# Three row blocks at once at the opening of the product of w3 and w_out2

## The chip, the cores and the metric

One Trainium2 chip, one core. The metric is the device time of one execution in microseconds, the median of several runs. Profiles show one execution; their times count from the first instruction. TensorE, VectorE, ScalarE, GpSimd and SyncE are PE, DVE, ACT, POOL and SP in the rows, PEld is TensorE's weight load.

## The reference

```python
attn_out = _attn_ref(q, k, v, g_q, g_k)     # 4 batches, 12 heads, 448 tokens, 64 wide; RMS norm on q and k, softmax
x = attn_out.transpose(0, 2, 1, 3).reshape(1792, 768)
x = relu(x @ moe_w_in) ** 2 @ moe_w_out     # 768 -> 2048 -> 768
a, b = x @ w1, x @ w2                       # 768 -> 1024
out = ((a * b) @ w3) @ w_out                # w3 1024 x 1024, w_out 1024 x 768
```

q, k and v are float32. The weights are float64 in memory.

## The kernel before

The two last products are one: w3 and the last w_out (wo2 in the code) are multiplied first, w3o = w3 @ w_out2, and each batch then uses w3o. The kernel goes through the 48 heads one after another (4 batches of 12), and beside each head's attention it issues matmuls of a second stream, paced by a credit: during heads 0 to 12 these are the 384 matmuls of w3o, and afterwards, for each batch, the 1008 matmuls of its MoE layers. The function fill(n) adds n to the credit and draws steps of three matmuls from a generator (gen_w3o, then gen_moe) until the credit is used. There are six such calls in a head. After head 12 the rest of w3o is drawn, and the first batch's MoE begins.

Products are made with numbers split in two: a float32 value is a high part (a rounded copy) and a low part (the value less the high part), and mm3 issues three matmuls, high by high, high by low, low by high (lines 262 to 264).

A weight comes in units of 128 partitions by 384 or 512 columns. The list `units` gives their order, and every step on a unit runs through the list in this order: load (SyncE; a float64 unit goes into one of four raw64 buffers, line 180), words (the high word on ScalarE, line 194, the low word on GpSimd or ScalarE, lines 198 and 200), join (VectorE makes a float32 of both, line 207, and frees the raw64 buffer), split_hi (ScalarE, line 106) and split_lo (GpSimd or VectorE, line 114). Which engine does the low word and the low part goes by the unit's number modulo 3 and 5 in the w3o product. advance(u) brings all of these up to unit u and a few units beyond: low parts to u + 2, high parts one unit further, joins to two and words to three units beyond the low parts, loads to five.

For w3o the units are 16 of w3 (two for each of 8 row blocks, four 128 x 128 pieces each) and 16 of wo2 (8 pieces jc by two halves of the columns, 384 wide). gen_w3o makes one row block after another, first half 0 of its columns, then half 1. The first row block therefore brings all 16 wo2 units with it, and these stay: two in the pool of x, eight in that of act, six in that of x2. Those of w3 go through the pool hl with four buffers. The sum of a row block and half, eight steps, is in a PSUM buffer of the pool ps_mm, which has three. ScalarE copies it to one of two osb buffers (copy_on, line 106), and SyncE stores that to w3o (line 289).

The order of instructions on each engine is made when the program is built, by a scheduler that follows the program's order where it expects operands to be ready and goes around what it expects to wait. On the chip each engine then keeps its order.

At the start SyncE issues the loads of the first k and q group, q_t of heads 0 to 2, v of heads 0 and 1 and the first two units; all later units follow with the first call of fill.

Of the kernel before, what the change touches and what calls it, by code (L numbers as in the profile page):

```python
# [8 lines left out]
F32 = mybir.dt.float32  # L9
F32R = mybir.dt.float32r  # L10
# [19 lines left out]
def attention_moe_kernel(  # L30
# [22 lines left out]
    NE = w_out.shape[0] // 4  # L53
    KF = w_out.shape[2] // 64
    NJ = w1.shape[0] // 2
    NIC = w3t.shape[0] // 2
    HC = KX * 128 // 2
    ENGS = {"v": nc.vector, "g": nc.gpsimd}
    KCS = ((0, 128), (128, 128), (256, 128), (384, 64))
# [44 lines left out]
    def copy_on(eng, out, in_):  # L104
        if eng == "a":
            nc.scalar.activation(out=out, in_=in_, func=AF.Copy)  # L106
        elif eng == "g":
            nc.gpsimd.tensor_scalar(out=out, in0=in_, scalar1=1.0, scalar2=1.0, op0=ALU.mult, op1=ALU.mult)
        else:
            nc.vector.tensor_copy(out=out, in_=in_)  # L110
# [10 lines left out]
    units = []  # L121
    wo_at, w3_at = {}, {}

    def add_wo(half, g):
        for j in range(NIC // 2):
            jc = g * NIC // 2 + j
            wo_at[half, jc] = len(units)
            units.append((wo2[jc, half], None))

    def add_w3(i):  # L130
        w3_at[i] = len(units)
        units.append((w3t[i], None))

    add_w3(0)
    add_wo(0, 0)
    add_w3(1)
    add_wo(0, 1)
    add_wo(1, 0)
    add_wo(1, 1)
    for i in range(2, 2 * NIC):  # L140
        add_w3(i)
    U0 = len(units)
    wo_units = set(wo_at.values())
    def two_first(n, on=True):
# [42 lines left out]
    def load_to(i):  # L187
        while pos["load"] <= min(i, NU - 1) and is64(pos["load"]):
            load_next()
# [27 lines left out]
    def split_hi(i):  # L217
        n = units[i][0].shape[-1]
        if i in wo_units:
            k = pos["wo"]  # L220
            pos["wo"] += 1
            p, nm = (xp, "x") if k < 2 else ((actp, "act") if k < 10 else (x2p, "x2"))
            t = p.tile([128, 2, S], F32R, name=nm, tag=nm)
        else:
            t = hlp.tile([128, 2, 512], F32R, name="hl", tag="hl")
        copy_on("a", t[:, 0, :n], raws[i][:, :n])
        hls[i] = t
# [27 lines left out]

    def use(u):
        advance(u)
        return hls.pop(u).rearrange("p a (k m) -> p a k m", m=128)

    def mm3(ps, w, wk, x, i, n):  # L260
        last = n - 1
        nc.tensor.matmul(ps, w[:, 0, wk, :], x[0], start=(i == 0), stop=False)  # L262
        nc.tensor.matmul(ps, w[:, 0, wk, :], x[1], start=False, stop=False)  # L263
        nc.tensor.matmul(ps, w[:, 1, wk, :], x[0], start=False, stop=(i == last))  # L264

    def hl_pair(t, n=S):
        return (t[:, 0, :n], t[:, 1, :n])
# [2 lines left out]
    wo = {}  # L270

    def gen_w3o():
        for ic in range(NIC):
            ws = None
            for half in range(2):
                ps = ps_mm.tile([128, 512], F32, name="mm", tag="mm")
                for jc in range(NIC):
                    if ws is None or jc * 2 // NIC >= len(ws):
                        ws = (ws or []) + [use(w3_at[2 * ic + len(ws or [])])]
                    if ic == 0:  # L280
                        advance(wo_at[half, jc])
                        wo[half, jc] = hls.pop(wo_at[half, jc])
                    w = ws[jc * 2 // NIC]
                    mm3(ps[:, :HC], w, jc % (NIC // 2), hl_pair(wo[half, jc], HC), jc, NIC)
                    yield 3
                o = t2.tile([128, S], F32, name="osb", tag="osb")
                copy_on("a", o[:, :HC], ps[:, :HC])
                k, c = divmod(ic, NIC // 2)
                nc.sync.dma_start(
                    out=w3o.rearrange("(e k) p (c m) -> e k p c m", k=2, m=128)[half * 3:half * 3 + 3, k, :, c, :]  # L290
                    .rearrange("e p m -> p e m"),
                    in_=o[:, :HC].rearrange("p (e m) -> p e m", m=128),
                )


    xs = {}
# [364 lines left out]
    nc.sync.dma_start(out=g_sb, in_=g_in)  # L661
    load_group(0)
    load_head(1)
    make_identity(nc, ident)
    nc.vector.tensor_copy(out=ident_r, in_=ident)
    nc.vector.scalar_tensor_tensor(
# [7 lines left out]
    start_fill(gen_w3o(), W3O)  # L674
    first.close()
    for h in range(NH + 1):
        n = W3O / ((H + 1) * 6) if h <= H else MOE / (H * 6)
        load_head(h + 3)
        load_v(h + 1)
        if h % GH == 0:  # L680
            load_group(h // GH + 1)
        stage_qk(h, 0)
        fill(n)
        stage_exp(h, 0)
        if h % H != 1:
            stage_x(h - 2)
        stage_t(h - 1, 0)
        stage_t(h - 1, 1)
        fill(n)
        stage_lo(h - 1)  # L690
        if h < NH:
            v_prep(h)
        fill(n)
        stage_k(h + 1)
        stage_t(h - 1, 2)
        stage_t(h - 1, 3)
        fill(n)
        stage_lo(h - 1)
        stage_qk(h, 1)
        fill(n)  # L700
        stage_exp(h, 1)
        fill(n)
        stage_v(h - 1)
        if h % GH == 1:
            group_prep(h // GH + 1)
        head_prep(h + 2)
        if h and h % H == 0:
            fill(1e9)
            stage_x(h - 1)
            start_fill(gen_moe(h // H - 1), MOE)  # L710
# [57 lines left out]
```

## Time and profile before

| | us |
|---|---|
| median of 3 runs | 1234.7 |
| lowest and highest | 1232.09, 1235.27 |
| the profiled execution | 1234.55 |
| its span, first to last instruction | 1232.8 |

The span leaves out 1.75 us around the instructions. The profiled execution lies 0.15 us under the median.

### The profile page before, as it was taken

The numbers are of one execution on the slowest core, as the hardware profiler recorded it, in microseconds if no ns is written. First come the engines' busy times: TensorE is split into PE (matmuls) and PEld (weight loads), VectorE is DVE, ScalarE is ACT, GpSimd is POOL, SyncE is SP. The second block draws the span as 40 slices with busy tenths as digits, with TensorE's granted clock in tenths as the row PEclk, the third lists the DMA queues.
The fourth block names the chain that finished last, engine by engine and source line by source line (L and its number), as shares of the span: only waits on it lengthen the run. The fifth ranks groups of instructions, "written<-read, shape, count | busy, mean of one in ns | idle before, by whom it ended". The sixth has DMA issues, their size and how long they took to land.

```text
span 1232.8 us, 18950 instructions
## 1 busy us (share of the span) xinstructions
PE 1160.9 (94%) x6192; PEld 1049.3 (85%) x6192; DVE 709.7 (58%) x1314; ACT 728.5 (59%) x1553; POOL 781.3 (63%) x772
## 2 busy tenths in 40 slices
PE   3789999998989899999999999999999999999998
PEld 2578888886878789998998998999999999999998
DVE  6699879768978774646567555655664421012100
ACT  5889876767657565656645555656545554343342
POOL 5875534655676655766776764856766556678673
PEclk9999999999998999999999999999999999999999
DMA  7774557888888755555535455544544443333342
GB/s 218 244 238 151 165 146 226 276 283 264 251 264 257 234 180 179 146 148 145 151 118 161 139 169 158 143 142 127 154 123 120 138 138 113 107 116 102 104 125 75
DMA packets 111347, 207.63 MB, mean 168 GB/s; under 512 B 12208, under 2 KB 66704, under 8 KB 111248
## 3 DMA queue, kind: packets, MB, share of 16 engines
q1 hardware_dynamic: 107792, 200.92, 54.0%
q10 hardware_dynamic: 3456, 5.51, 1.2%
q8 instruction: 49, 0.80, 0.3%
q14 instruction: 50, 0.41, 0.1%
HBM read 149.95 MB, written 27.53 MB: 144 GB/s over the span
## 4 chain that ended last, share of the span: by engine, by line
PE 60%; DMA 4%; DVE 2%; POOL 2%; ACT 1%; issue 1%; SPq 0%; DVEq 0%; POOLq 0%; ACTq 0%
PE mm L262 17%; PE mm L263 17%; PE mm L264 17%; PE kv L622 3%; PE pt L570 3%; DMA raw<-w 2%; DMA pw<-p 2%; PE sc L525 1%; PE sc L524 1%; POOL hl L114 1%; DVE raw L207 1%; PE kv L508 1%; PE mm L611 0%; ACT p L543 0%; POOL x L114 0%
## 5 line engine op out<-in xcount | busy, mean ns | idle before, releaser
L114 POOL TENSOR_TENSOR hl<-raw,hl 128x384 fp32r<-128x384 f32 (+1 forms) x383 | 446.4, 1169 | 258.5 <-ACT hl L106 253.3
L106 ACT ACTIVATE hl<-raw 128x384 fp32r<-128x384 f32 (+1 forms) x416 | 233.7, 564 | 147.6 <-PE mm L264 85.6
L263 PE MATMUL mm<-x,hl 128*128 128x448 f32 (+1 forms) x832 | 306.2, 368 | 8.6 <-POOL x L114 8.6
L262 PE MATMUL mm<-x,hl 128*128 128x448 f32 (+1 forms) x832 | 310.5, 373 | 3.8 <-ACT x L106 1.8
L264 PE MATMUL mm<-x,hl 128*128 128x448 f32 (+1 forms) x832 | 305.7, 367 | 4.5 <-POOL hl L114 2.6
L263 PE MATMUL mm<-act,hl 128*128 128x448 f32 (+1 forms) x640 | 234.4, 366 | 3.3 <-POOL act L114 3.2
L262 PE MATMUL mm<-act,hl 128*128 128x448 f32 (+1 forms) x640 | 236.9, 370 | 0.0
L264 PE MATMUL mm<-act,hl 128*128 128x448 f32 (+1 forms) x640 | 233.6, 365 | 0.7 <-DVE hl L114 0.7
L543 ACT ACTIVATE p<-sc,nb,rr 112x448 f32<-112x448 f32 x192 | 137.4, 719 | 86.4 <-DVE nb L527 83.0
L263 PEld LDWEIGHTS mm<-x,hl 128*128 128x128 f32 x832 | 158.1, 190 | 22.1 <-POOL x L114 10.2
L264 PEld LDWEIGHTS mm<-x,hl 128*128 128x128 f32 x832 | 158.2, 190 | 19.0 <-POOL hl L114 4.0
L262 PEld LDWEIGHTS mm<-x,hl 128*128 128x128 f32 x832 | 157.9, 190 | 18.5 <-ACT x L106 3.3
L526 DVE TENSOR_REDUCE nb<-sc 112x1 f32<-112x448 f32 x192 | 113.1, 615 | 35.6 <-PE sc L525 34.3
L263 PEld LDWEIGHTS mm<-act,hl 128*128 128x128 f32 x640 | 121.0, 189 | 14.3 <-POOL act L114 4.8
L264 PEld LDWEIGHTS mm<-act,hl 128*128 128x128 f32 x640 | 120.9, 189 | 10.6 <-DVE hl L114 1.1
L262 PEld LDWEIGHTS mm<-act,hl 128*128 128x128 f32 x640 | 121.0, 189 | 9.4
L114 DVE TENSOR_TENSOR ptr<-pt,ptr 128x448 fp32r<-128x448 f32 x144 | 87.1, 619 | 72.0 <-ACT ptr L106 71.4
L200 POOL TENSOR_SCALAR raw<-raw 128x384 uint32<-128x384 uint16 (+1 forms) x110 | 82.1, 747 | 73.0 <-DMA raw<-w_in 18.8
L207 DVE SCALAR_TENSOR_TENSOR raw<-raw 128x384 uint32<-128x384 uint32 (+1 forms) x120 | 84.8, 711 | 39.8 <-POOL hl L114 25.2
L194 ACT ACTIVATE raw<-raw 128x384 f32<-128x384 f32 (+1 forms) x120 | 70.5, 597 | 53.9 <-DMA raw<-w 18.0
L114 POOL TENSOR_TENSOR act<-gf,act 128x448 fp32r<-128x448 f32 x80 | 97.4, 1218 | 7.2 <-DVE gf L334 3.0
L334 DVE TENSOR_TENSOR gf<-mm,r 128x448 f32<-128x448 f32 x64 | 39.8, 621 | 94.4 <-ACT r L330 93.9
(82 smaller groups left out, 1588.7 us busy)
## 6 DMA issues: line engine op xcount, KB each, us to landing
pw<-p SPq DMA_DIRECT2D x72, 392.0 KB, 4.3
raw<-f_in SPq DMA_DIRECT2D x96, 192.0 KB, 2.4
raw<-f_out SPq DMA_DIRECT2D x72, 256.0 KB, 2.7
raw<-f SPq DMA_DIRECT2D x96, 192.0 KB, 2.4
raw<-w_in SPq DMA_DIRECT2D x32, 384.0 KB, 4.5
raw<-w_out SPq DMA_DIRECT2D x24, 512.0 KB, 6.1
raw<-w SPq DMA_DIRECT2D x32, 384.0 KB, 4.9
raw<-w3o SPq DMA_DIRECT2D x48, 256.0 KB, 2.7
```

Of the source, the lines that this page charges most:

```text
L106: nc.scalar.activation(out=out, in_=in_, func=AF.Copy)
L114: e.tensor_tensor(out=out, in0=in0, in1=in1, op=ALU.subtract)
L194: nc.scalar.activation(out=hi, in_=hi, func=AF.Prelu, scale=2.0**-112, alpha=-(2.0**32))
L200: nc.gpsimd.tensor_scalar(out=t[:, :n, 0], in0=low, scalar1=2.0**-13, scalar2=2.0**-14 - 0.5, op0=ALU.mult, op1=ALU.add)
L207: nc.vector.scalar_tensor_tensor(out=f[:, :n].bitcast(U32), in0=t[:, :n, 1], scalar=3, in1=t[:, :n, 0], op0=ALU.logical_shift_left, op1=AL ...
L262: nc.tensor.matmul(ps, w[:, 0, wk, :], x[0], start=(i == 0), stop=False)
L263: nc.tensor.matmul(ps, w[:, 0, wk, :], x[1], start=False, stop=False)
L264: nc.tensor.matmul(ps, w[:, 1, wk, :], x[0], start=False, stop=(i == last))
L334: nc.vector.tensor_tensor(out=gf, in0=ps, in1=r, op=ALU.mult)
L526: nc.vector.tensor_reduce(out=nb[:, j:j + 1], in_=o[j], axis=AX.X, op=ALU.max, negate=True)
L543: nc.scalar.activation(out=p, in_=o[j], func=AF.Exp, scale=d["rq"][:, c:c + 1], bias=nb[:, j:j + 1], accum_out=sm[:, i, c:c + 1],)
L570: nc.tensor.transpose(to[:kn, c * P:(c + 1) * P], d["p"][c][:, k0:k0 + kn], one)
```

## The change

The w3o product opens with three row blocks at once. For half 0 of the columns, step jc of rows 0, 1 and 2 follow each other, so one wo2 unit serves nine matmuls instead of three; then the same for half 1; rows 3 to 7 follow one by one as before. The units stand in the order in which this uses them: w3 units of three rows between the wo2 units of half 0, then the wo2 units of half 1, then the other w3 rows. Rows 0 and 1 are cut into units of 3, 3 and 2 pieces, the other rows in 4 and 4, which makes 34 units. The six units of rows 0 and 1 go to the pool of x, the wo2 units to act (eight), x2 (six) and x (two). Units 2 and 3 are loaded right after q_t of head 1. The credit is 4.5 for each call in heads 0 and 1 and 5.0 for each in heads 2 to 12, instead of 4.92 in all.

```diff
-    NIC = w3t.shape[0] // 2
+    NIC = w3t.shape[0]
+    NR = 3
...
+    def add_w3(ic, a, b):
+        for jc in range(a, b):
+            w3_at[ic, jc] = (len(units), jc - a)
+        units.append((w3t[ic][:, a * 128:b * 128], None))
+
+    CUTS = [(0, 3, 6, 8)] * (NR - 1) + [(0, 4, 8)] * (NIC - NR + 1)
+    for jc in range(NIC):
+        for ic in range(NR):
+            if jc in CUTS[ic][:-1]:
+                add_w3(ic, jc, CUTS[ic][CUTS[ic].index(jc) + 1])
+            if ic == 0:
+                add_wo(0, jc)
+    for jc in range(NIC):
+        add_wo(1, jc)
+    early = {w3_at[ic, jc][0] for ic in range(NR - 1) for jc in range(NIC)}
+    for ic in range(NR, NIC):
+        for a, b in zip(CUTS[ic], CUTS[ic][1:]):
+            add_w3(ic, a, b)
...
-            p, nm = (xp, "x") if k < 2 else ((actp, "act") if k < 10 else (x2p, "x2"))
+            p, nm = (actp, "act") if k < 8 else ((x2p, "x2") if k < 14 else (xp, "x"))
             t = p.tile([128, 2, S], F32R, name=nm, tag=nm)
+        elif i in early:
+            t = xp.tile([128, 2, S], F32R, name="x", tag="x")
...
+        ws = {}
+
+        def rows(ics, half):
+            pss = [ps_mm.tile([128, 512], F32, name="mm", tag="mm") for _ in ics]
+            for jc in range(NIC):
+                for ic, ps in zip(ics, pss):
+                    u, i = w3_at[ic, jc]
+                    if u not in ws:
+                        ws[u] = use(u)
                     if ic == 0:
                         advance(wo_at[half, jc])
                         wo[half, jc] = hls.pop(wo_at[half, jc])
+                    mm3(ps[:, :HC], ws[u], i, hl_pair(wo[half, jc], HC), jc, NIC)
+                    if jc == NIC - 1:
+                        o = t2.tile([128, S], F32, name="osb", tag="osb")
+                        copy_on("a", o[:, :HC], ps[:, :HC])
...
                     yield 3
+
+        for half in range(2):
+            yield from rows(range(NR), half)
+        for ic in range(NR, NIC):
+            for half in range(2):
+                yield from rows([ic], half)
...
     load_head(1)
+    load_to(3)
...
-        n = W3O / ((H + 1) * 6) if h <= H else MOE / (H * 6)
+        n = (9 * NR if h < 2 else (W3O - 18 * NR) / (H - 1)) / 6 if h <= H else MOE / (H * 6)
...
-        "w3t": units(w3.T, 4),
+        "w3t": units(w3.T, 8),
```

## Rows read from the trace of the kernel before

**Rows 1.** Head of the page: the span, and each engine's busy time.
```profile
span 1232.8 us, 18950 instructions
...
PE 1160.9 (94%) x6192; PEld 1049.3 (85%) x6192; DVE 709.7 (58%) x1314; ACT 728.5 (59%) x1553; POOL 781.3 (63%) x772
```

**Rows 2.** Windows: stretch, length, busy us and instructions by engine, clock, DMA, GB/s.
```profile
5.00:10.00 5.00, 0.49 (x4) 0.49 (x4) 3.05 (x12) 2.47 (x5) 2.77 (x4) 1.00 1.00 311
...
core 0: us, PE busy (x) PEld busy (x) DVE busy (x) ACT busy (x) POOL busy (x), PEclk, DMA share, GB/s
...
20.00:60.00 40.00, 26.01 (x104) 19.00 (x105) 25.38 (x41) 31.02 (x68) 33.87 (x37) 0.96 0.70 223
60.00:100.00 40.00, 36.02 (x218) 31.67 (x216) 39.37 (x69) 35.81 (x76) 28.68 (x31) 1.00 0.68 218
...
190.00:460.00 270.00, 242.97 (x1269) 215.75 (x1268) 217.63 (x383) 175.21 (x381) 166.08 (x179) 0.97 0.79 249
460.00:1232.80 772.80, 767.40 (x4079) 704.05 (x4077) 335.15 (x599) 404.84 (x858) 502.92 (x459) 1.00 0.45 134
```

**Rows 3.** Waits from 20 to 60 us: us in total, times, longest.
```profile
PE mm L263 <- POOL x L114: 5.9, 3, 2.9
...
DVE nb L526 <- PE sc L525: 8.0, 6, 2.0
```

**Rows 4.** Timeline of TensorE: start, duration; L524 is a head's scores.
```profile
32.99 0.57 PE L524 MATMUL sc<-kt,qh 128*112 128x448 f32 x1
...
56.19 0.43 PE L524 MATMUL sc<-kt,qh 128*112 128x448 f32 x1
...
58.33 0.34 PE L262 MATMUL mm<-act,hl 128*128 128x384 f32 x1
...
59.29 0.44 PE L264 MATMUL mm<-x,hl 128*128 128x384 f32 x1 [0.45 <-POOL hl L114]
...
59.74 0.34 PE L263 MATMUL mm<-x,hl 128*128 128x384 f32 x1
59.92 0.35 PE L264 MATMUL mm<-x,hl 128*128 128x384 f32 x1
...
97.25 0.38 PE L524 MATMUL sc<-kt,qh 128*112 128x448 f32 x1
```

**Rows 5.** SyncE: issues of loads in order of time, and its waits from 10 to 70.
```profile
14.56 0.35 SPq L414 DMA_DIRECT2D qt<-q_t  x1
14.96 1.37 SPq L180 DMA_DIRECT2D raw<-wo  x3
...
25.32 10.08 SPq L180 DMA_DIRECT2D raw<-wo  x6
...
62.89 2.03 SPq L180 DMA_DIRECT2D raw<-w3t  x2
...
SPq L180 <- DVE raw L207: 35.7, 18, 6.8
```

**Rows 6.** Windows of one line: L262 (one for each step), then L207 (joins).
```profile
0.00:56.18 56.18, 7.46 (x16) 3.83 (x16) 0.97 0.75 234
...
0.00:56.18 56.18, 13.29 (x19) 0.97 0.75 234
0.00:97.20 97.20, 21.59 (x29) 0.98 0.72 225
```

**Rows 7.** Groups of VectorE from 60 to 100: count, busy us, mean ns.
```profile
L207 DVE SCALAR_TENSOR_TENSOR raw<-raw 128x512 uint32<-128x512 uint32 x9 | 7.6, 846 | 0.2 <-ACT raw L198 0.2
...
L114 DVE TENSOR_TENSOR hl<-raw,hl 128x512 fp32r<-128x512 f32 x2 | 2.0, 1000 | 0.0
```

**Rows 8.** Joins up to 100 us: ns least, median, most; starts; forms.
```profile
L207 DVE SCALAR_TENSOR_TENSOR raw<-raw x29: 544/678/1297, 10.3 to 96.2; 128x384 uint32<-128x384 uint32 x16, 128x512 uint32<-128x512 uint32 x13
```

**Rows 9.** Timelines of ScalarE and GpSimd: the first exponential, the first use of v.
```profile
18.99 0.72 ACT L543 ACTIVATE p<-sc,nb,rr 112x448 f32<-112x448 f32 x1 [5.68 <-DVE nb L527]
...
17.16 1.58 POOL L114 TENSOR_TENSOR vhl<-v,vhl 128x256 fp32r<-128x256 f32 x2 [1.78 <-DVE nt L432]
```

**Rows 10.** First result of w3o: copy, issue of its store, time to landing.
```profile
41.67 0.49 ACT L106 ACTIVATE osb<-mm 128x384 f32<-128x384 f32 x1 [0.62 <-PE mm L264]
...
44.81 0.43 SPq L289 DMA_DIRECT2D w3o<-osb  x1
...
w3o<-osb SPq DMA_DIRECT2D x1, 192.0 KB, 3.8
```

More of the change, by code (lines that the diff above doesn't have):

```diff
@@ L122, in attention_moe_kernel, with add_wo @@
     wo_at, w3_at = {}, {}
[L124 to L141, printed above, removed]
+    def add_wo(half, jc):
+        wo_at[half, jc] = len(units)
+        units.append((wo2[jc, half], None))
+    def add_w3(ic, a, b):
[15 more added lines that the diff above has]
+            add_w3(ic, a, b)
     U0 = len(units)
@@ L257, in use @@
         advance(u)
-        return hls.pop(u).rearrange("p a (k m) -> p a k m", m=128)
+        return hls.pop(u)[:, :, :units[u][0].shape[-1]].rearrange("p a (k m) -> p a k m", m=128)
     def mm3(ps, w, wk, x, i, n):
@@ L272, in gen_w3o @@
     def gen_w3o():
[L273 to L279, printed above, removed]
+        ws = {}
[6 more added lines that the diff above has]
+                        ws[u] = use(u)
                     if ic == 0:
@@ L282, in gen_w3o @@
                         wo[half, jc] = hls.pop(wo_at[half, jc])
-                    w = ws[jc * 2 // NIC]
-                    mm3(ps[:, :HC], w, jc % (NIC // 2), hl_pair(wo[half, jc], HC), jc, NIC)
-                    yield 3
[L286 to L293, printed above, removed]
+                    mm3(ps[:, :HC], ws[u], i, hl_pair(wo[half, jc], HC), jc, NIC)
+                    if jc == NIC - 1:
+                        o = t2.tile([128, S], F32, name="osb", tag="osb")
+                        copy_on("a", o[:, :HC], ps[:, :HC])
+                        k, c = divmod(ic, NIC // 2)
+                        nc.sync.dma_start(
+                            out=w3o.rearrange("(e k) p (c m) -> e k p c m", k=2, m=128)
+                            [half * 3:half * 3 + 3, k, :, c, :].rearrange("e p m -> p e m"),
+                            in_=o[:, :HC].rearrange("p (e m) -> p e m", m=128),
+                        )
+                    yield 3
+        for half in range(2):
[3 more added lines that the diff above has]
+                yield from rows([ic], half)
     xs = {}
```

## The prediction

> **What bounds the kernel now.** I read the time by stage first. One engine sets the end: from 460 us to the last instruction TensorE is busy 767.40 of 772.80 us, so whatever is won or lost earlier arrives at the end whole [rows 1, 2]. Before that it is not full: 26.01 of 40 us between 20 and 60, 36.02 of 40 between 60 and 100, 242.97 of 270 between 190 and 460 [rows 2]. The change acts in the first two of these stretches, and in them other engines are nearer their limit: GpSimd has 33.87 of 40 us up to 60, VectorE 39.37 of 40 from 60 to 100 [rows 2]. The reader should see a handover: conversion of weights holds the opening, VectorE the heads after it, TensorE the rest.
>
> The waits of TensorE between 20 and 60 say what it misses: 5.9 us for the low part of a weight unit, made on GpSimd (POOL x) [rows 3]. Its timeline gives the milestones: first scores of head 1 at 32.99 us, of head 2 at 56.19, of head 5 at 97.25 [rows 4]. So heads 0 and 1 need far longer than the 41.06 us / 3 = 13.7 us that heads 2 to 4 take each. At 56.19 only 16 of the 128 steps (three matmuls each) of the w3 product have been issued, and 19 units joined [rows 6]; the matmuls follow each other at about 0.18 us where nothing is missing [rows 4]. TensorE is starved, not slow.
>
> Who feeds it? SyncE's queue. The four raw64 buffers are a ring: a load waits until an earlier unit's join on VectorE frees a buffer, 35.7 us in 18 waits [rows 5]. From the load at 25.32 to the end of the last of the pair at 62.89 + 2.03 there are 21 loads, so one unit per (64.92 - 25.32) / 21 = 1.89 us. That is the pace of the opening.
>
> **The change part by part.** *Same work.* The 384 matmuls, their columns and the weight bytes stay. Rows 0 and 1 of w3 come as three units each where they were two, so 34 units instead of 32. Two units more, with no more columns: their fixed part on VectorE. A join of 384 columns takes 0.544 us at the least [rows 8]; the narrow units replace columns that were joined anyway, so I charge a third of it each and round the pair to 0.4 us. Bounds: 0 and two full joins at 0.846 [rows 7], 1.7 us. They are conversions whose cover (GpSimd and ScalarE, neither full) remains.
>
> *Fewer units ahead of head 2.* In the old order 12 pacing calls of 384 / 78 = 4.92 matmuls stand ahead of head 2's first scores: 59 matmuls, so 20 steps, the last 4 of them in row 1. Step 20 uses unit 18 (numbers from 0), and with the lookahead of 2 that makes 21 units split. In the new order the same 12 calls give 54 matmuls, 18 steps, jc 0 to 5 of three rows; these use units up to 11, with the lookahead 14 units. Seven units less, at the ring's pace 7 x 1.89 = 13.2 us earlier. The scheduler does not hold the program's order strictly (16 steps were issued at 56.19 where the program's order has 20 [rows 6]), so this is an estimate. Bounds: 0, if a head's own chain of scores, maximum, exponential and transposes holds the opening, and 13.2. I take 13.2 because TensorE's longest waits are for units and the ring is what SyncE waits for [rows 3, 5]. The matmuls do not stand against it: with 14 units the new order has enabled 60 of them (jc 0 to 5 of three rows, and two rows of jc 6), the old order 36 (half 0 of row 0 and four steps of half 1).
>
> *The seven units come back.* They are then due in heads 2 to 4, where VectorE is full. One costs it 0.846 us for the join and, one time in five, 1.000 us for a low part [rows 7]: 1.05 us. Seven are 7.3 us, with the fixed part above 7.7 us to be paid back. Bounds: 0, if they fall into the gaps that are left, and the ring's price again, 13.2 us. I take VectorE's because that engine has 0.6 us free in those 40 [rows 2]. ScalarE's share of a unit is hidden: it has 4.2 us free there, and a wait on it would show as exponentials late.
>
> *Units 2 and 3 ahead.* Before, units 2 to 5 are issued from 14.96 on, behind a q_t load that waits for its buffer [rows 5]. Now two of them go out behind the q_t load of head 1, with all four raw64 buffers free. ScalarE sits idle 5.68 us before the first exponential at 18.99 [rows 9], room for two units' conversions. That is at best two places in the ring, 3.8 us; GpSimd is near full after 20, so I take one, 1.9 us. The price: 384 + 512 KB at the 311 GB/s of that stretch [rows 2] hold the loads queued behind on SyncE (q_t of head 2, v of heads 0 and 1, the second group of k and q) 2.9 us. GpSimd's first use of v comes at 17.16 and waits there for VectorE [rows 9], so I cost it at nothing; without that cover it is 2.9 us on head 0's chain.
>
> *Three accumulators at once.* The pool ps_mm has three buffers; the new opening holds all three, and rows 0 to 2 end one step apart. Their results leave through two osb buffers, so the third copy waits for the first store. In the old trace the first copy begins at 41.67, its store is issued at 44.81 behind a waiting load and lands 3.8 us later [rows 10]: 48.61 - 41.67 = 6.9 us. Two steps (six matmuls of 0.18, 1.1 us) pass meanwhile, leaving up to 5.8 us at the handover from half 0 to half 1, and again from half 1 to row 3. Behind the waiting copy ScalarE's exponentials are queued, and behind those VectorE's and TensorE's work of the head. Before, copies lay 24 matmuls apart and this did not exist. Bounds 0 and 2 x 5.8 = 11.6 us. The scheduler goes round a matmul that is not ready (at 58.33 it issues the next step's before the one at 59.29 that waits for its low part [rows 4]), and the third row alone is late, so I take the low end, 1.5 us for both.
>
> A sentence of the Trainium skill bears on this. Perfetto Trace Analysis, Optimization Strategy, says that a gap repeating on the engine that should be saturated can mean that there is not enough PSUM for the next tile to be allocated; by that the handover would be paid twice in full, and the sum below would end as in the third rival.
>
> *Engines of the conversions* shift, since they go by the unit's number modulo 3 or 5: equal in number in the opening, and in the first MoE batch a pattern of three that starts one place over. No sign; bound by a low part on VectorE, 1.0 us a time [rows 7], in a stretch with waits of its own. I carry 3 us both ways for that stretch.
>
> **Sum.** -13.2 + 7.7 - 1.9 + 1.5 = -5.9 us. Against the profiled execution's own 1234.55 us (span 1232.8) that is 1228.7 us; the median of the runs, 1234.7, is 0.15 above that execution, so it stands for the median too. A measurement of this kernel can tell about 0.3%, 3.7 us, from no change.
>
> **The rivals.**
> *Paid back in full.* The joins become dearer as GpSimd's low parts move in beside them. For it: a join takes between 0.544 and 1.297 us in the first 100 us, 0.678 in the middle [rows 8]. Against: the mean in the full stretch is 0.846 already [rows 7]. Between heads 2 and 5 the old kernel joins 10 units (29 less 19 [rows 6]); the new one 17. Every second at 1.297 costs 17 / 2 x 0.45 = 3.8 us: 1232.5 us.
> The Trainium skill has a rule of this kind. SBUF — State Buffer, Who interferes with whom, says that a VectorE instruction with two SBUF inputs and a GpSimd instruction that reads SBUF exclude each other, the second waiting in full. By it every one of the 17 would pay, 7.7 us, and the time would be 1236.3 us.
> *The opening is held by the heads' own chains*, so that the new order brings nothing: about 1234.5 us. For it: VectorE waits 8.0 us for scores between 20 and 60 [rows 3]. Against: TensorE itself and SyncE wait for units there [rows 3, 5].
> *Slower, by the handover.* With 5.8 us at both, the sum is -5.9 + 11.6 - 1.5 = +4.2 us, 1238.8 us. It decides once a handover stalls above 3.7 us (no gain left), and gives slower beyond 0.3% from about 5.6 us each. For it: two osb buffers against three rows. Against: attention matmuls lie between.
> *More than forecast.* The moved units fit into gaps, since half 1 and row 3 need few; pay-back 3 us, both early units count: -13.2 + 3 - 3.8 + 1.5 = -12.5 us, 1222 us.
>
> **How the numbers follow.** Forecast 0.45 (own range 1225 to 1232), paid back 0.18, own chains 0.10, slower by the handover 0.12, more than forecast 0.15. The predicted time is 1228.7. Faster by over 0.3%: most of the forecast, all of the last, a little of the pay-back, 0.55. Slower: the handover and the upper end of the pay-back, 0.16. Within: the rest, 0.29. For the range, the 1222 of the largest gain with the 3 us of the MoE stretch gives 1219, and the handover's 1239 closes it above; beyond lie the extremes of several bounds at once.
>
> **What would show it.** Head 2's first scores near 45 us instead of 56.19, with at most 16 joins by then: the first term. Heads 2 to 4 at 15 us each or more, VectorE full in them, head 5 near 91: the pay-back. Loads of units 2 and 3 issued by 8 us and joined before 20: the third. A ScalarE copy to osb that waits for a store, and TensorE waiting for it after the 72nd and 144th w3 matmul: the handover. Between 460 and the end TensorE must still be full. The prediction is wrong if head 2 starts before 50 but head 5 no earlier than 95, or if the stretch of the first MoE batch changes by more than 3 us.

## The result and the profile after

The changed kernel takes 1247.76 us (median of 4 runs, 1244.2 to 1253.13) where the kernel before takes 1234.66 (4 runs, 1232.09 to 1235.27): ratio 1.0111, 95% interval 1.0081 to 1.0142. The forecast was 1228.7 us in a range of 1219 to 1239: wrong in sign, and outside the range. The profiled execution took 1245.89 us, its span is 11.3 us longer than before's.

The head of the page, beside [rows 1]: one row of busy time for each engine.

```profile
span 1244.1 us, 18957 instructions
...
PE 1170.0 (94%) x6192; PEld 1056.4 (85%) x6192; DVE 713.9 (57%) x1315; ACT 727.6 (58%) x1558; POOL 794.6 (64%) x776
```

There are 7 instructions more in 18950. TensorE is busy 9.1 us longer with the same 6192 matmuls, GpSimd 13.3 us longer with four more instructions, VectorE 4.2 us with one more, ScalarE no longer at all: the same work, made dearer, rather than added work. Where it arises is read from TensorE's timeline of the changed kernel, at the first scores (L539) of heads 2, 3, 5, 8 and 13; columns are start, duration, engine, line, operation.

```profile
50.51 0.37 PE L539 MATMUL sc<-kt,qh 128*112 128x448 f32 x1
...
70.09 0.37 PE L539 MATMUL sc<-kt,qh 128*112 128x448 f32 x1
...
95.34 0.46 PE L539 MATMUL sc<-kt,qh 128*112 128x448 f32 x1
...
129.36 0.46 PE L539 MATMUL sc<-kt,qh 128*112 128x448 f32 x1
...
199.00 0.46 PE L539 MATMUL sc<-kt,qh 128*112 128x448 f32 x1 [1.60 <-ACT p L558]
```

Head 2 starts 5.7 us earlier than before (56.19 in [rows 4]), head 3 6.6 us earlier (before 76.7), head 5 only 1.9 us earlier (97.25), head 8 2.3 us earlier (131.62), and head 13 10.1 us later (188.87). The opening did win. The loss lies behind it, between heads 5 and 13, where of the whole change only the credit of 5.0 and the shifted numbers act: 103.66 us, 12.0 more than before's 91.62. The windows between these milestones, first of the changed kernel, beside [rows 2]; columns as there.

```profile
0.00:50.50 50.50, 28.13 (x108) 21.24 (x109) 32.85 (x79) 31.06 (x66) 32.17 (x43) 1.00 0.73 225
50.50:95.34 44.84, 37.44 (x205) 33.01 (x204) 40.13 (x75) 37.58 (x85) 36.71 (x38) 0.89 0.67 207
95.34:199.00 103.66, 91.74 (x533) 81.95 (x532) 89.29 (x180) 78.71 (x171) 49.93 (x59) 0.95 0.53 151
199.00:470.00 271.00, 243.31 (x1262) 214.22 (x1263) 214.51 (x382) 173.45 (x378) 172.36 (x178) 0.97 0.79 249
470.00:1244.00 774.00, 769.37 (x4089) 705.96 (x4087) 337.15 (x601) 406.75 (x862) 503.42 (x459) 1.00 0.45 134
```

And the window of heads 5 to 12 of the kernel before:

```profile
97.25:188.87 91.62, 85.42 (x527) 77.19 (x526) 79.79 (x178) 74.56 (x165) 41.28 (x54) 1.00 0.55 162
```

The third row of the first fence against this one is the case in little. The instructions are nearly as many (TensorE 533 and 527, VectorE 180 and 178, ScalarE 171 and 165). TensorE is 6.2 us idle before and 11.9 after, and its granted clock was 1.00 and is 0.95. VectorE needs 9.5 us more for two more instructions. Of the 12.0 us, 5.7 are idle time of TensorE and 6.3 a longer busy time. From head 13 to the end both take the same within 1.2 us (1043.9 and 1045.1), and from 470 us on TensorE is full at clock 1.00.

What TensorE and ScalarE wait for from head 5 to head 13 (total us, times, longest). The changed kernel:

```profile
ACT qn L465 <- DMA kn<-k_nat: 5.5, 1, 5.5
ACT raw L199 <- DMA raw<-w_in: 4.3, 2, 3.4
...
ACT qn L465 <- DMA qn<-q_nat: 2.4, 1, 2.4
...
PE sc L539 <- ACT p L558: 5.6, 5, 3.5
PE kv L523 <- DVE xf L645: 2.0, 2, 1.2
PE pt L585 <- DVE ptr L115: 1.9, 3, 0.9
```

The kernel before, in the same heads:

```profile
ACT qn L450 <- DMA kn<-k_nat: 3.6, 1, 3.6
...
ACT qn L450 <- DMA qn<-q_nat: 1.9, 1, 1.9
...
PE sc L524 <- ACT p L543: 5.1, 5, 1.6
```

Two waits of TensorE of the kernel before, 0.6 and 0.4 us, are not shown.

ScalarE waits 12.2 us for loads (k, q and units of w_in, the first MoE layer) where it waited 5.5. Since its order is fixed, an exponential queued behind such an instruction waits with it, and TensorE behind the exponential. The plainest place is at head 12: ScalarE's square of the next group's k (L465) and TensorE's first scores of that head, in the changed kernel and then in the kernel before.

```profile
182.81 1.06 ACT L465 ACTIVATE qn<-kn 112x1024 f32<-112x1024 f32 x1 [5.54 <-DMA kn<-k_nat]
...
184.63 0.71 PE L539 MATMUL sc<-kt,qh 128*112 128x448 f32 x1 [3.53 <-ACT p L558]
```

```profile
176.22 1.06 ACT L450 ACTIVATE qn<-kn 112x1024 f32<-112x1024 f32 x1 [3.64 <-DMA kn<-k_nat]
...
178.04 0.46 PE L524 MATMUL sc<-kt,qh 128*112 128x448 f32 x1 [1.62 <-ACT p L543]
```

In head 8 lies another place, where TensorE is held by a different engine. The changed kernel's timelines of VectorE, GpSimd and TensorE:

```profile
134.59 1.24 DVE L542 TENSOR_TENSOR nb<-nb,rr 112x2 f32<-112x2 f32 x1
135.76 0.61 DVE L115 TENSOR_TENSOR ptr<-pt,ptr 128x448 fp32r<-128x448 f32 x1
...
134.54 1.27 POOL L115 TENSOR_TENSOR hl<-raw,hl 128x512 fp32r<-128x512 f32 x1
...
133.75 0.50 PE L523 MATMUL kv<-ident_r,khl 112*128 112x112 f32 x4 [0.76 <-DVE xf L645]
134.72 0.60 PE L585 MATMUL pt<-ident,p 112*128 112x112 f32 x4 [0.47 <-DVE ptr L115]
...
136.42 0.95 PE L585 MATMUL pt<-ident,p 112*64 112x112 f32 x4 [0.92 <-DVE ptr L115]
...
137.84 0.52 PE L269 MATMUL mm<-act,hl 128*128 128x384 f32 x1
138.16 0.52 PE L270 MATMUL mm<-act,hl 128*128 128x384 f32 x1
...
140.56 0.33 PE L269 MATMUL mm<-act,hl 128*128 128x384 f32 x1
140.73 0.33 PE L270 MATMUL mm<-act,hl 128*128 128x384 f32 x1
```

TensorE pauses three times (0.76, 0.47, 0.92 us), each time for VectorE, which works there without a gap. The last pause ends with the instruction on ptr that stands behind a product of 2 columns a partition (nb, L542). This product took 1.24 us and ended with a low part on GpSimd (134.54 + 1.27), where one with no GpSimd instruction beside it takes 0.14 to 0.16 us (last section). ScalarE waits 2.38 us for a load of q at the same time, but the exponential behind it needs that product, so it could not have started before 135.83 in any case; it started at 136.35. After the pauses w3 matmuls of the same shape follow each other at 0.32 us until about 139.7, at 0.17 us later. The windows behind the two places of the changed kernel say why:

```profile
136.30:139.70 3.40, 3.28 (x12) 3.12 (x13) 2.96 (x7) 2.83 (x8) 1.75 (x2) 0.50 0.86 239
184.10:190.90 6.80, 6.27 (x24) 5.74 (x25) 4.58 (x11) 5.15 (x13) 0.71 (x2) 0.50 0.42 116
```

Granted clock 0.50, the lower of its two levels (1.2 GHz), with TensorE busy 3.28 of 3.40 and 6.27 of 6.80 us: slow, not starved.

The Trainium skill, TensorE: Matmul & The Clock Gate, Part 1, says that a gate sets the clock to one of these two levels by how busy the engine has been; the rows agree in that both falls come right behind pauses.

An estimate from the two rows of heads 5 to 12: TensorE's waits there sum to 10.2 us after (with two of 0.5 and 0.2 not shown) and 6.1 before, 4.1 more; a mean clock of 0.95 over 103.7 us costs at most 0.05 x 103.7 = 5.2 us against none at 1.00. Together 9.3 of the 12.0 us. The two places alone come to nearly as much: 2.2 us of pauses in head 8, 1.9 more than before at head 12, and at most half of the 3.4 and 6.8 us at the lower clock, 5.1, make 9.2.

### The profile page after: what moved, and what is told of

It reads as the page before. It is cut to its first block, busy times and chain, and to the rows that moved or that the text cites. A ratio compares the mean times of both kernels' runs of the same rounds, so it can differ in the third digit from the quotient of the medians.

```text
span 1244.1 us, 18957 instructions
## 1 busy us (share of the span) xinstructions
PE 1170.0 (94%) x6192; PEld 1056.4 (85%) x6192; DVE 713.9 (57%) x1315; ACT 727.6 (58%) x1558; POOL 794.6 (64%) x776
## 4 chain that ended last, share of the span: by engine, by line
PE 62%; DVE 12%; DMA 10%; POOL 7%; issue 4%; ACT 4%; SPq 1%; DVEq 0%; POOLq 0%; ACTq 0%
PE mm L269 17%; PE mm L270 17%; PE mm L271 17%; PE pt L585 3%; PE kv L637 3%; POOL hl L115 2%; DVE raw L212 2%; DVE nb L541 2%; DMA raw<-w_out 2%; PE sc L539 2%; PE sc L540 2%; DMA pw<-p 2%; DMA raw<-w_in 2%; ACT p L558 1%; POOL raw L205 1%
## 5 line engine op out<-in xcount | busy, mean ns | idle before, releaser
L107 ACT ACTIVATE hl<-raw 128x384 fp32r<-128x384 f32 (+1 forms) x412 | 231.2, 564 | 149.6 <-PE mm L271 85.2
L269 PE MATMUL mm<-x,hl 128*128 128x448 f32 (+1 forms) x816 | 304.6, 373 | 1.0 <-DVE gf L349 1.0
L270 PE MATMUL mm<-x,hl 128*128 128x448 f32 (+1 forms) x816 | 300.7, 369 | 1.6 <-POOL x L115 1.6
L271 PE MATMUL mm<-x,hl 128*128 128x448 f32 (+1 forms) x816 | 300.5, 368 | 0.7 <-POOL hl L115 0.7
L271 PE MATMUL mm<-act,hl 128*128 128x448 f32 (+1 forms) x624 | 228.7, 366 | 3.1 <-POOL hl L115 3.1
L269 PE MATMUL mm<-act,hl 128*128 128x448 f32 (+1 forms) x624 | 231.3, 371 | 0.0
L270 PE MATMUL mm<-act,hl 128*128 128x448 f32 (+1 forms) x624 | 228.5, 366 | 0.0
L270 PEld LDWEIGHTS mm<-x,hl 128*128 128x128 f32 x816 | 155.5, 191 | 13.9 <-POOL x L115 1.9
L269 PEld LDWEIGHTS mm<-x,hl 128*128 128x128 f32 x816 | 155.1, 190 | 14.2 <-DVE gf L349 1.4
L271 PEld LDWEIGHTS mm<-x,hl 128*128 128x128 f32 x816 | 155.2, 190 | 14.0 <-POOL hl L115 1.5
L205 POOL TENSOR_SCALAR raw<-raw 128x384 uint32<-128x384 uint16 (+2 forms) x111 | 86.5, 779 | 78.2 <-DMA raw<-w_in 33.8
L271 PEld LDWEIGHTS mm<-act,hl 128*128 128x128 f32 x624 | 118.1, 189 | 13.9 <-POOL hl L115 4.6
L269 PEld LDWEIGHTS mm<-act,hl 128*128 128x128 f32 x624 | 118.0, 189 | 9.4
L270 PEld LDWEIGHTS mm<-act,hl 128*128 128x128 f32 x624 | 118.3, 190 | 8.9
L212 DVE SCALAR_TENSOR_TENSOR raw<-raw 128x384 uint32<-128x384 uint32 (+2 forms) x122 | 85.7, 708 | 44.2 <-POOL hl L115 24.1
L199 ACT ACTIVATE raw<-raw 128x384 f32<-128x384 f32 (+2 forms) x122 | 70.9, 592 | 59.3 <-DMA raw<-w_in 17.3
L539 PE MATMUL sc<-kt,qh 128*112 128x448 f32 x192 | 77.2, 402 | 27.7 <-ACT p L558 25.1
```

Source lines behind the costliest of these rows:

```text
L199: nc.scalar.activation(out=hi, in_=hi, func=AF.Prelu, scale=2.0**-112, alpha=-(2.0**32))
L205: nc.gpsimd.tensor_scalar(out=t[:, :n, 0], in0=low, scalar1=2.0**-13, scalar2=2.0**-14 - 0.5, op0=ALU.mult, op1=ALU.add)
L212: nc.vector.scalar_tensor_tensor(out=f[:, :n].bitcast(U32), in0=t[:, :n, 1], scalar=3, in1=t[:, :n, 0], op0=ALU.logical_shift_left, op1=AL ...
L539: nc.tensor.matmul(o[j], d["qh"][:, c * P:(c + 1) * P], d["kt"], start=True, stop=False)
```

## The experiments

Theories were formed one after another, and each set of runs was to tell two or more apart. *Numbers*: the two added units shift which engine does which conversion of the later units. *Credit*: 5.0 in heads 2 to 12 instead of 4.92 sets the loss. *Put-off*: the work that the opening shed comes back in heads 5 to 12. *Queue*: ScalarE stands before loads that are late. *Order*: any small edit makes the scheduler build another order of the whole opening and of heads 5 to 12, better or worse by about 1%, and the loss is no cost of any one part. The table gives for each kernel the first scores of heads 2, 5 and 13 on TensorE, the stretch from 5 to 13, what ScalarE waited for loads in it (each from one profiled execution, in us), the granted clock of that stretch, and the ratio to the kernel before in runs on the same chip.

| kernel | head 2 | head 5 | head 13 | 5 to 13 | ScalarE on loads | clock | ratio, 95% |
|---|---|---|---|---|---|---|---|
| before | 56.2 | 97.3 | 188.9 | 91.6 | 5.5 | 1.00 | 1 |
| after | 50.5 | 95.3 | 199.0 | 103.7 | 12.2 | 0.95 | 1.0111 (1.0081 to 1.0142) |
| e1_numbers | 51.9 | 99.3 | 204.5 | 105.2 | 16.1 | 0.95 | 1.0082 (1.0053 to 1.0112) |
| e2_pace | 52.7 | 96.4 | 192.2 | 95.8 | 3.7 | 0.98 | 1.0054 (1.0036 to 1.0071) |
| e3_numbers_pace | 50.9 | 92.6 | 189.0 | 96.4 | 7.7 | 1.00 | 1.0007 (0.9992 to 1.0022) |
| e4_no_early_load | 53.2 | 97.3 | 199.3 | 102.0 | 11.5 | 0.97 | 1.0106 (1.008 to 1.0132) |
| b1_pace | 58.8 | 101.0 | 200.0 | 99.1 | 13.9 | 0.98 | 1.0065 (1.0042 to 1.0088) |
| b2_numbers | 58.1 | 97.3 | 190.3 | 92.9 | 2.4 | 1.00 | 1.0008 (0.9996 to 1.0021) |
| b3_numbers_pace | 57.0 | 95.8 | 188.6 | 92.8 | 4.2 | 1.00 | 1.0002 (0.9988 to 1.0016) |
| b4_early_load | 53.9 | 102.3 | 194.8 | 92.5 | 5.5 | 1.00 | 1.0034 (1.002 to 1.0049) |
| c1_words_later | 54.7 | 96.4 | 195.2 | 98.8 | 5.2 | 0.97 | 1.0075 (1.0056 to 1.0095) |
| c2_groups_earlier | 50.9 | 96.5 | 199.7 | 103.2 | 9.0 | 0.95 | 1.0102 (1.0074 to 1.0129) |
| q1_before_485 | 58.5 | 100.8 | 195.3 | 94.6 | 7.6 | 1.00 | 1.0053 (1.0031 to 1.0075) |
| q2_after_485 | 53.9 | 95.6 | 191.9 | 96.3 | 8.7 | 0.98 | 1.0107 (1.0087 to 1.0127) |
| d1_two_rows | 55.7 | 94.0 | 196.6 | 102.6 | 10.6 | 0.95 | 1.0048 (1.0029 to 1.0068) |
| d2_all_old_words_later | 60.0 | 98.2 | 200.8 | 102.7 | 11.6 | 0.95 | 1.007 (1.0046 to 1.0095) |
| d3_before_words_later | 61.9 | 101.5 | 201.1 | 99.6 | 11.4 | 0.97 | 1.0078 (1.0058 to 1.0097) |

The clock sorts the stretch with little overlap: at 1.00 it takes 91.6 to 96.4 us (six kernels), at 0.98 95.8 to 99.1 (three), at 0.97 98.8 to 102.0 (three), at 0.95 102.6 to 105.2 (five). The longest single pause of TensorE in the stretch goes with it: 2.9 us or more in eight of the nine kernels of 98.8 us or longer (1.9 in b1_pace, the ninth), 2.6 or less in the eight shorter ones. In seven of those eight that pause is for an exponential, and ScalarE had come out of a wait of about 3.5 us or more for a load 1.3 to 2.6 us before TensorE went on; in e1_numbers it is for VectorE.

**The parts of the change undone.** The first: the changed kernel, with the engines of units from 24 on chosen by the number that the unit had before.

```diff
+    def num(i):
+        return i if i < 24 else i - 2
...
-low_eng[i % len(low_eng)]
+low_eng[num(i) % len(low_eng)]
-lo_eng[i % len(lo_eng)]
+lo_eng[num(i) % len(lo_eng)]
```

> The changed kernel, but every unit from the fourth w3 row on takes its engines by the number it had before the change (two less). Numbers theory: the changed kernel loses its lead of 2.2 us at head 8 and falls 10.1 us behind by head 13 because low parts that were on VectorE are now on GpSimd (7 against 4 in those heads) and its small instructions stand behind them (nb product 490 ns against 184). Then this kernel keeps the lead through head 13 and takes 1232 to 1236 us. Pace theory (5.0 matmuls for each call instead of 4.92 shift the order of heads 8 to 12) or opening theory (three rows at once leave the engines in a worse order for good): no change, 1244 to 1252 us.

Measured 1246.83 us. The stretch is no shorter (105.2): undoing the numbers alone does not undo the loss.

The second: the changed kernel with the old credit of 4.92.

```diff
-        n = (9 * NR if h < 2 else (W3O - 18 * NR) / (H - 1)) / 6 if h <= H else MOE / (H * 6)
+        n = W3O / ((H + 1) * 6) if h <= H else MOE / (H * 6)
```

> The changed kernel with the old credit of 4.92 for every call in heads 0 to 12. Pace theory: heads 8 to 13 take again about 57 us (70 in the changed kernel), 1232 to 1238 us. Numbers theory and opening theory: 1244 to 1252 us.

Measured 1242.84 us: head 13 at 192.2 instead of 199.0, about half of the loss gone. The edit takes back both parts of the credit, 4.5 in heads 0 and 1 and 5.0 behind them. The prediction counted the first as fewer matmuls ahead of head 2, and what the credit does to the order behind that it priced at nothing.

The third: both of these diffs.

> The changed kernel with both: old numbers for the engines of the units from the fourth row on, and the old credit. Numbers theory or pace theory or both: 1230 to 1236 us. If it stays at 1244 to 1252 us, neither is the cause, and the order that three rows at once leave behind is what remains.

Measured 1236.08 us (10 runs), no measurable difference from before. Undoing both removes the loss, though one alone makes no clear difference and the other takes away half. Head 5 comes at 92.6, 4.6 us ahead of before, and head 13 at 189.0, level with before: the new opening alone wins 4.6 us, and heads 5 to 12 take it back. The window of heads 5 to 12 of this kernel, and what TensorE waits for in it:

```profile
92.60:189.00 96.40, 86.99 (x535) 77.90 (x534) 85.87 (x181) 79.23 (x172) 47.00 (x57) 1.00 0.59 170
```

```profile
PE sc L542 <- ACT p L561: 7.5, 7, 2.4
```

The clock stays at 1.00 here. TensorE's waits (9.3 us with three of 0.3 to 1.0 not shown) are 3.2 above before's 6.1, of 4.8 that the stretch is longer, and most are for exponentials.

The fourth: the changed kernel without `load_to(3)`.

> The changed kernel without the early load of units 2 and 3. By the prediction's third term the early load is worth 1.9 us, so 1.9 us later at head 2 than the changed kernel; the time at the end then tells how far an opening that is 2 us later goes through to the end: 1248 to 1250 us if it goes through whole, anything from 1234 to 1252 us if the order that the scheduler makes after the opening decides more than the opening itself.

Measured 1248.68 us. Head 5 is 1.9 us later than in the changed kernel, and head 2 2.7: the early load is worth about what it was priced at. At the end 0.9 us is left of it, less than the noise.

**The parts put into the kernel before.** The credit of the change (4.5, then 5.0) in the old order; the numbers shifted (`num(i) = i if i < 22 else i + 2`); both; `load_to(3)` after `load_head(1)`.

```diff
-        n = W3O / ((H + 1) * 6) if h <= H else MOE / (H * 6)
+        n = (27 if h < 2 else (W3O - 54) / (H - 1)) / 6 if h <= H else MOE / (H * 6)
```

> The kernel before, its old opening kept, with the new credit alone (4.5 for each call in heads 0 and 1, 5.0 in heads 2 to 12). Pace theory (the credit of 5.0 makes a worse order of heads 8 to 12 whatever the opening): 1240 to 1247 us, with heads 8 to 13 over 62 us. Rival, the three rows and the credit hurt only together: 1233 to 1237 us.

> The kernel before, with the engines of the units from the fourth row on taken by numbers two higher, as the change makes them. Numbers theory: 1238 to 1246 us, most of it lost between heads 8 and 13, with fewer low parts on VectorE there. Rival, the numbers matter only in the changed order: 1233 to 1237 us.

> The kernel before with both the new credit and the new numbers, none of the three rows, no early load. If credit and numbers are the whole loss, 1244 to 1250 us. If the loss needs the new opening, under 1240 us.

> The kernel before with units 2 and 3 loaded early and nothing else. The prediction's third term, measured as 2.0 us at head 5 in the changed order, would give 1232 to 1234 us if a lead of the opening reaches the end. Rival, work put off or done earlier evens out before head 13: 1235 to 1237 us at the end, whatever the lead at head 5.

Measured 1245.23, 1237.14, 1237.36 and 1241.48 us. The credit alone costs the old opening 0.65%, and with the numbers shifted as well it costs nothing: the effects of the two don't add there. In the new opening undoing them gained 0.3% and 0.6% one by one and 1.0% together, which adds up within the noise. The early load brings head 2 forward by 2.3 us and leaves head 5 5 us behind, outside what was expected of it. The waits of b1_pace from head 5 to head 13 show, without any of the new opening, waits like those of the changed kernel: ScalarE 13.9 us on loads, and TensorE on exponentials. The place is another one, though: heads 5 to 7 take 39.8 us instead of 34.4, and heads 8 to 12 59.3, not the over 62 that was expected of them.

```profile
ACT raw L194 <- DMA raw<-w_in: 10.5, 6, 2.9
ACT qn L450 <- DMA kn<-k_nat: 2.2, 1, 2.2
ACT qn L450 <- DMA qn<-q_nat: 1.2, 1, 1.2
...
PE sc L524 <- ACT p L543: 5.9, 6, 1.6
```

**The queue, from two sides.** In the changed kernel the words of units are drawn one unit later, so that ScalarE reaches a unit of w_in later; and separately the loads of k and q groups are issued two heads earlier.

```diff
-    WORD_AHEAD = 3
+    WORD_AHEAD = 2
```

```diff
-        if h % GH == 0:
-            load_group(h // GH + 1)
+        if h == 0:
+            load_group(1)
+        if h % GH == 2:
+            load_group((h + 2) // GH + 1)
```

> The changed kernel with the words of a unit made two units ahead of its low part instead of three, so a load has one unit's time more to land before ScalarE and GpSimd turn to it. Queue theory: between heads 5 and 13 ScalarE, which keeps its order, stands 12.2 us before loads that have not landed (w_in units 4.3 us, k and q groups 7.9) with exponentials behind them, against 5.5 in the kernel before. Then its waits for w_in fall to under 2 us, heads 5 to 13 take under 99 us (103.7 in the changed kernel) and the time is 1238 to 1244 us. Rival, the waits on loads are only where the lost time shows and something else sets the pace: waits fall, the stretch stays at 102 to 105 us.

> The changed kernel with each later group of k and q loaded two heads earlier. Queue theory: ScalarE's waits for k and q fall from 7.9 us to under 3, heads 5 to 13 take under 100 us, the time is 1239 to 1244 us. Rival as above: the stretch stays at 102 to 105 us and the time at 1245 us or more.

Measured 1243.84 and 1246.76 us. The first shortens the stretch to 98.8 us and ScalarE's waits on loads to 5.2. But 4.2 of them are on w_in, where under 2 was expected and where it was 4.3 without the edit: what went away are waits for k and q, which the edit was not aimed at. The second leaves both nearly as they were (103.2 and 9.0), because it moved no load. The issue of one k load in the changed kernel, and then in this one (a q load likewise, 129.62 and 130.50):

```profile
177.84 0.33 SPq L420 DMA_DIRECT2D kn<-k_nat  x1
...
179.02 0.33 SPq L420 DMA_DIRECT2D kn<-k_nat  x1
```

The k load goes out when GpSimd's last instruction on the buffer's old keys (kx) has ended, at 177.81 in the changed kernel, and lands 5.0 us later; an earlier place in the program did not change that. So neither edit took away the waits that it was aimed at, and whether loads that come earlier would shorten the stretch is not tested by them.

**The size of the credit.** 4.85 in all calls of heads 0 to 12, in the old order and in the new.

```diff
+        n = 4.85 if h <= H else MOE / (H * 6)
```

> The kernel before with a credit of 4.85 instead of 4.92 in heads 0 to 12, a change that moves a step of three matmuls by at most one call. Order theory (the stretch from head 5 to head 13 swings by several us with any small change of the order): anything from 91 to 100 us in that stretch, 1234 to 1246 us, and where it is above 97 us ScalarE's waits for loads are above 9 us. Rival, the credit must be large to hurt: 1233 to 1236 us.

> The changed kernel with a credit of 4.85 in heads 0 to 12. Order theory: 93 to 106 us from head 5 to head 13, 1235 to 1249 us, long where ScalarE's waits for loads are long. Rival, three rows at once are slower by themselves: 1243 us or more with the old numbers missing here, whatever those waits are.

Measured 1239.4 and 1248.28 us. A smaller credit is no cure: in the old order 4.85 costs 0.53%, and 4.5 with 5.0 (b1_pace) 0.65%, against the 4.92 of the kernel before. In the new order head 13 comes at 191.9, better than after, and the loss moves behind it: from head 13 to the end 1055.2 us against 1043.9 before. By itself this run does not rule out its rival, that three rows are slower by themselves; e3_numbers_pace, at 1.0007, does.

**A smaller opening, and words later elsewhere.** Two rows at once, all rows in two units (so no added units), old credit; e3_numbers_pace with WORD_AHEAD 2; the kernel before with WORD_AHEAD 2.

```diff
-    NR = 3
+    NR = 2
-    CUTS = [(0, 3, 6, 8)] * (NR - 1) + [(0, 4, 8)] * (NIC - NR + 1)
+    CUTS = [(0, 4, 8)] * NIC
-    early = {w3_at[ic, jc][0] for ic in range(NR - 1) for jc in range(NIC)}
+    early = set()
```

> Two row blocks at once instead of three, no narrow units (32 units, so old numbers), old credit, early load kept; the w3 units stay in the pool hl. Put-off theory (the lead of the opening is partly work put off: two more units, one group sum, and it is paid between heads 5 and 13): with no more units than before and a smaller lead at head 5 (1 to 4 us), it reaches head 13 with 188 to 192 us and takes 1232 to 1238 us. Rival, several rows at once cost by themselves in the later heads: heads 5 to 13 above 96 us and 1238 us or more.

> Three rows at once with the old credit, the old engine numbers and the words one unit later. Queue theory: ScalarE's waits for loads between heads 5 and 13, 7.7 us with the first two alone, fall under 5, the stretch falls from 96.3 to 92 or 94 us, and the time is 1231 to 1234 us, under the kernel before. Rival, order theory (each such edit throws the order anew): 92 to 104 us and 1233 to 1246 us with no tie to the first two edits.

> The kernel before with the words one unit later. Queue theory: ScalarE waits only 5.5 us for loads there, none of it for units, so nothing is gained: 1233 to 1236 us. Order theory: 1233 to 1246 us.

Measured 1242.88, 1246.39 and 1245.8 us. With two rows, no added unit and no changed credit, head 5 is 3.2 us ahead and head 13 7.8 us behind, so put-off units of the change are not needed for the loss; the outcome is the one that the rival had named. The edit that helped c1_words_later costs the old opening 0.78% and, against 1.0007 without it, e3's opening 0.6%. ScalarE's waits in d2_all_old_words_later from head 5 to head 13 have only moved from w_in to k and q:

```profile
ACT qn L468 <- DMA kn<-k_nat: 6.5, 1, 6.5
ACT qn L468 <- DMA qn<-q_nat: 4.6, 1, 4.6
```

No edit of the queue, in any of these four kernels, took the waits away as a whole or gave a kernel faster than the one before. What is left is order: the seven kernels with the old opening lie between 1 and 1.0078, the ten with a new one between 1.0007 and 1.0111, and what an edit costs depends on the others beside it. None beats the kernel before: of "better or worse" only the worse half was seen.

## Why the prediction was wrong, point by point

*The first term*, -13.2, is at most 5.7 by measurement (head 2 at 50.51 instead of 56.19), and that with the early load in it: without the load (e4_no_early_load) head 2 comes at 53.2, 3.0 us ahead. The sign is right, the size is not. Joins up to head 2, and steps (L269), of the changed kernel, beside [rows 6]:

```profile
0.00:50.50 50.50, 8.14 (x15) 1.00 0.73 225
...
0.00:50.50 50.50, 7.38 (x19) 4.36 (x19) 1.00 0.73 225
```

15 units joined instead of 19, and 19 steps issued instead of 16. So four units, not seven, separate the two: the old trace's own 19 joins were the count to subtract from, and the prediction put the program order's 21 in their place. Four at the ring's 1.89 us make 7.6, still above the 3.0; and TensorE goes on waiting for GpSimd's low parts between 20 and 60, 4.6 us in the longest row against 5.9 in [rows 3] (with the smaller rows 6.8 against 9.5), so the ring was not all that held it:

```profile
PE mm L270 <- POOL act L115: 4.6, 2, 3.5
```

*The pay-back*, 7.7, is 3.8 in length, but not by its mechanism: heads 2 to 4 take 44.8 us instead of 41.06, with 14 joins in place of 10. VectorE, whose full time was to be the price, is busy only 0.9 us longer (40.13 and 39.20) and idle 4.7 us instead of 1.9. What fell is TensorE's clock, 0.89 against 1.00, at most 0.11 x 44.8 = 4.9 us, more than the whole 3.8. It fell behind 9.5 us in which TensorE was busy 4.53 (50.5 to 60.0), to a mean of 0.60 in the 10.1 us after them. The window of the kernel before, beside the second row above:

```profile
56.18:97.25 41.07, 36.23 (x218) 31.78 (x217) 39.20 (x70) 36.85 (x77) 30.43 (x32) 1.00 0.68 214
```

With the same new opening and a clock of 0.96 there, e3_numbers_pace takes 41.7 us for these heads, with 13 joins. So the moved units cost little, and head 5 at 95.34 lies behind the 91 expected because of the first term and the clock. The joins of that window by width, in the changed kernel and then in the kernel before (count, busy us, mean ns):

```profile
L212 DVE SCALAR_TENSOR_TENSOR raw<-raw 128x384 uint32<-128x384 uint32 x9 | 7.4, 818 | 1.5 <-ACT raw L203 0.8 <-POOL raw L205 0.6
L212 DVE SCALAR_TENSOR_TENSOR raw<-raw 128x512 uint32<-128x512 uint32 x5 | 3.4, 678 | 0.0
```

```profile
L207 DVE SCALAR_TENSOR_TENSOR raw<-raw 128x512 uint32<-128x512 uint32 x10 | 8.3, 829 | 0.2 <-ACT raw L198 0.2
```

The narrow joins are dearer than the least of 544 ns in [rows 8], one of them 2.82 us long, and the wide ones cheaper than before. All fourteen take 10.8 us, less than 14 at the 846 ns of [rows 7], so the rival that made joins dearer has its mechanism in some of them and not its price. By the Trainium skill's rule on the port that VectorE and GpSimd share (SBUF — State Buffer, Who interferes with whom), as the prediction used it, every join would have paid; the five wide ones did not.

*The early load*, -1.9: e4_no_early_load reaches head 5 1.9 us later. Right in size for the new order; in the old one b4_early_load ends 5 us behind at head 5, so the price holds for that order alone.

*The handover of three accumulators*, +1.5, and the rival with 5.8 us twice: nothing in the changed kernel. What ScalarE waited for ahead of a copy to osb from head 5 to head 13 (ahead of head 5 there is none):

```profile
ACT osb L107 <- PE mm L271: 0.5, 1, 0.5
ACT osb L107 <- PE sc L540: 0.2, 1, 0.2
```

No copy waited for a store there. The wait exists in other orders of the same opening: one copy waited 2.1 us in e2_pace (at 66), 1.5 in q2_after_485 and 0.4 in d2_all_old_words_later, so the low end was the right choice and the order decides whether it is paid. The one rival that ended slower has the right side for a wrong reason. The Trainium skill's reading of a repeating gap as missing buffers (Perfetto Trace Analysis, Optimization Strategy), which would have paid the handover twice in full, is not borne out here; no run paid it more than once or more than 2.1 us.

*The sum to head 5* was -5.9, and -1.9 was measured: the sizes were off, the direction right. The step that failed is the next one, "whatever is won or lost earlier arrives at the end whole". That sentence rests on TensorE being full from 460 us on [rows 2], and from head 13 on it held within 1.2 us (271.00 us from 199 to 470 with TensorE busy 243.31, like the 270 with 242.97); in the other kernels that part takes 1040.7 to 1048.7 us, 1055.2 in q2_after_485. It says nothing of the stretch from head 5 to head 13, where TensorE had 6.2 us idle and VectorE was busy 79.79 of 91.62: tight, and led by an order that the scheduler makes anew for any edit. There a lead of 1.9 us became a deficit of 10.1, by the pauses and the two falls of the clock shown above; no term allowed for either. The signs of being wrong that the prediction named watch heads 2 to 4 and the first MoE batch, and not this stretch. The prediction had the place in view, as "engines of the conversions shift", with "no sign" and 3 us both ways. The numbers shift by itself is indeed near nothing (b2_numbers 1.0008); what the bound left out is the credit, which costs 0.65% by itself in the old opening (b1_pace) and nothing beside shifted numbers (b3_numbers_pace).

What is shown: the opening wins (4.6 us at head 5 with old credit and numbers, 1.9 with new); in none of the ten kernels with a new opening does head 13 come before the 188.87 of the kernel before (189.0 to 204.5); credit and numbers undone together give 1.0007, each alone does not; in the old opening the credit alone gives 1.0065 and with the numbers 1.0002. The traces also show by what the changed kernel loses: two pauses and the lower clock behind them are some 9 of the 12 us, one pause behind ScalarE's wait for a load, the other behind VectorE. What is only argued: that the other kernels lose by the same chain. For it: the clock and the longest pause sort the stretch as said above, and ScalarE's waits on loads are at most 5.5 us in the four kernels whose stretch is under 94 us, and 9.0 or more in all eight of 99 us or longer. Against it, e1_numbers has its longest pause for VectorE, e2_pace has 95.8 us with waits of 3.7, b1_pace 99.1 us with no long pause, and no edit took the waits away alone. Which instruction, placed where, makes the new order worse stays open: each edit tried here moved many at once.

## What to carry to other kernels

A profile that shows the last two thirds saturated lets a gain arrive whole only if the stretch between the edit and that part is saturated too; where it isn't, ask what in it holds by chance. When a scheduler writes the order at build time, even a pacing constant changed by 1.4% (4.92 to 4.85, q1_before_485) can move a kernel by 0.53%, about as much as the planned gain of 6 us: measure the edit together with small variants of the pacing, and price the re-made order as a term of its own, here from nothing to some 10 us with the old opening (up to 1.0078), before pricing its parts. A gain seen at one milestone should be followed milestone by milestone to the end before it is called kept. And before an edit is read as a test, the trace should show that it moved what it was meant to move: c2_groups_earlier moved no load.

## What the runs showed of the hardware

A short run of pauses costs TensorE more than themselves: waits of 0.76, 0.47 and 0.92 us with matmuls in between were followed by 3.4 us at granted clock 0.50, in which matmuls stood 0.32 us apart instead of 0.17, and a single one of 3.53 us by 6.8 us at 0.50. The four runs of the changed kernel spread with that clock: mean granted clocks of 0.989, 0.985, 0.982 and 0.981 gave 1244.2, 1245.89, 1249.62 and 1253.13 us. That is no rule for every kernel: of 15 runs of the kernel before, the fastest (1232.22 us) had 0.986 and the slowest (1239.41) 0.989.

VectorE's small products of 2 columns a partition (nb, L527 before and L542 after) take 184 ns in heads 8 to 12 before and 490 after, with equal shapes; the changed kernel and then the kernel before:

```profile
L542 DVE TENSOR_TENSOR nb<-nb,rr 112x2 f32<-112x2 f32 x10 | 4.9, 490 | 0.0
```

```profile
L527 DVE TENSOR_TENSOR nb<-nb,rr 112x2 f32<-112x2 f32 x10 | 1.8, 184 | 0.0
```

The same instruction is cheap or dear by what runs beside it, and the timelines say what. Of the 32 products in heads 5 to 12 of the two kernels, 22 took 0.14 to 0.16 us. The other ten, 0.23 to 1.24 us, all began while a GpSimd instruction was running, and nine of them ended within 0.02 us of its end, as the one shown in the first section did. Three of the ten are in the kernel before and seven in the changed one, where GpSimd has more low parts to make in these heads (busy 49.93 us instead of 41.28). Joins of 384 columns went from a mean of 552 to 724 ns in heads 8 to 12, but several beside a GpSimd instruction took no longer than alone. The Trainium skill (SBUF — State Buffer, Who interferes with whom) names a port pair that VectorE and GpSimd share. The products agree with it and the joins only in part; no run here took GpSimd's work away from beside them.
